# The triangular inverse carried through the lower rows on GpSimd or VectorE, with one joining product on TensorE, and decay products that run over two chunks

## The chip, the cores and the metric

The kernel runs on one core of one Trainium2 chip. The metric is the device time of one execution in microseconds (us). The kernel before took 593.81 us, the median of three runs (589.45 to 594.18).

## The reference

For 4 batches, 8 heads, 768 steps and head size 40, a state matrix is carried step by step; what comes out goes through a layer norm and a two-layer network of width 320 to 1280 to 320 with a residual.

```python
for t in range(S):
    y[:, :, t] = np.einsum('bhd,bhde->bhe', rt, state)
    Sa = np.einsum('bhde,bhe->bhd', state, at)
    state_decay = state * wt[:, :, None, :] - np.einsum('bhd,bhe->bhde', Sa, bt)
    state = state_decay + np.einsum('bhd,bhe->bhde', vt, kt)
...
ch = np.maximum(xn @ w_ch1, 0.0) @ w_ch2
return x + ch
```

The decays `w` lie between 0.85 and 0.95. All is float32.

## The kernel before

Time is cut into 24 chunks of C = 32 steps; B = 16 is half a chunk. The 32 pairs of batch and head lie in two halves of the partitions. Within a chunk the recurrence becomes matrix products and the inverse of a unit lower triangle of 32 x 32 for each pair.

For each chunk c there are these steps. `prep(c)` loads the decays `wa` and the rows `bk`, makes running products of the decays in the chunk (VectorE scan L338 from the front into `gE`, reciprocal L340, scan L342 from the back into `qE`), multiplies them into `x2s` (L350) and `bk` (L356), and forms the 32 x 32 interactions on TensorE (L366). Their signed copy goes by DMA to DRAM (`d_l`). Steps L350 and L356 are on VectorE for chunks 0 and 1, later on GpSimd (POOL in the profile).

`invert(s)` works on a slab: chunk 0 alone, chunk 1 alone, then two chunks at a time (11 slabs of two). The triangles come back from `d_l` into the tile `yv`, one pair of batch and head on each partition, and both 16 x 16 blocks on the diagonal are inverted at the same time in 14 steps of two instructions (L416 multiplies, L420 adds). Slabs 0 and 1 do this on VectorE, the others on POOL. ScalarE (ACT) copies a transposed block (L422), DMAs write `d_h`, and `merge(c)` reads it back into `hv`. There TensorE joins the two blocks: a first product (L441) makes a 16-column piece, ACT copies it into `qm` (L443), and a second product (L452) gives the whole inverse, which ACT copies to `tt`.

`chain(c)` is the recurrence from chunk to chunk: L498 from the state `x2`, a copy on ACT, L508 with the inverse `tt`, four copies on ACT (L512), L523, and then VectorE adds the old state (L532) and scales the sum by the decay product of the next chunk (L533), four times each. `post(c)` forms the output of the chunk (L551, L563, L578, L595). `norm` and `moe` are the layer norm and the network: L766 and L750 are its two products, done for two chunks at a time: ten groups of 8 matmuls (L766) and ten of 6 (L750).

The order of all instructions is set before the program is built. `Plan.order` is given each step with its engine, a cost in us, a key (the chunk, with an offset) and what it reads and writes; it lays the steps out as a list scheduler would and issues them in that order. At run time each engine takes its instructions strictly in that order, and an instruction that waits holds up all that stand behind it on its engine. A change of a cost therefore moves other steps too.

Of the kernel before, what the change touches and what calls it, by code (L numbers as in the profile page):

```python
# [11 lines left out]
F32 = mybir.dt.float32  # L12
# [4 lines left out]
ALU = mybir.AluOpType  # L17
# [4 lines left out]
C = 32  # L22
B = C // 2
D = 40
# [158 lines left out]
def body(ctx, tc, ea, eb, vr, rd, vt, w1, w1x_in, w2, gl, fe, fd, out):  # L183
# [27 lines left out]
    start0, = ring(1, "start0", 16, 33)  # L211
# [7 lines left out]

    yv, = ring(1, "yv", 2 * 33 * B)  # L220
    tmp, = ring(1, "ytmp", 2 * 56)

    hv = ring(2, "hv", 8, 5 * B)
    qm, = ring(1, "qm", 8, C)
# [23 lines left out]
    d_h = [dr.tile([32 * n, B, 3 * B], F32, name=f"d_h{s}") for s, (_, n) in enumerate(SLABS)]  # L248
# [15 lines left out]
    def consts():  # L264
# [16 lines left out]
        for i in range(2):  # L281

            op("DVE", 0.9, -99 + i, (), [("wa", i, 0)], lambda i=i: V.memset(wa[i][32:64], 1.0))
        for i in range(BK):
            op("POOL", 0.9, -99 + i, (), [("bk", i, 0)], lambda i=i: G.memset(bk[i][32:64], 1.0))
        op("POOL", 0.3, -84, (), ["qm"], lambda: G.memset(qm, 0.0))
# [5 lines left out]
        def f():  # L292
            V.memset(start0, 2.0 ** -33)
            V.memset(start0[:, :, 0:1], 1.0)
            V.memset(last, 0.0)
        op("DVE", 1.0, -95, (), ["start0", "last"], f)
        op("ACT", 0.3, -95, (), [("small", 0)], lambda: (A.memzero(small[0]["sd"]), A.sqrt(small[0]["sd"], small[0]["sd"])))
        for i in range(2):
# [3 lines left out]
            def f(i=i):  # L302
                for q, qs in enumerate(QUADS):
                    up, lo = (ident[qs, 32 * q + B * x:32 * q + B * x + B].unsqueeze(1).broadcast_to([32, 8, B])
                              for x in range(2))
                    A.copy(out=hv[i][qs, :, 0:B], in_=lo)
                    A.copy(out=hv[i][qs, :, 4 * B:5 * B], in_=up)
                    if i == 0:
                        A.copy(out=qm[qs, :, 0:B], in_=lo)
            op("ACT", 2.6 if i == 0 else 1.8, -50 + i, ["ident"], two("hv", i, 4) + (["qm"] if i == 0 else []), f)  # L310
# [13 lines left out]
    def prep(c):  # L324
# [9 lines left out]
        for hf in (1, 0):  # L334
# [3 lines left out]
        op("DVE", 1.35, kp, W + ["start0"], [("g", i)], lambda: nc.vector.tensor_tensor_scan(  # L338
            out=flat(g[R]), data0=t[R, 0:n], data1=flat(start0[R]), initial=0.0, op0=ALU.mult, op1=ALU.max), lock=True)
        op("DVE", 0.29, kp, [("g", i)], ["last"], lambda: nc.vector.reciprocal(  # L340
            out=last[R, :, C:33], in_=g[R, :, C:33]))
        op("DVE", 1.4, kp, W + ["last"], [("q", i)] + ([("go",)] if c == 0 else []), lambda: nc.vector.tensor_tensor_scan(  # L342
            out=flat(q[R])[:, ::-1], data0=t[R, n:0:-1], data1=flat(last[R])[:, ::-1], initial=0.0,
            op0=ALU.mult, op1=ALU.max), lock=True)
# [624 lines left out]
```

## Time and profile before

| | before |
|---|---|
| runs, median (range) | 593.81 us (589.45 to 594.18) |
| the profiled execution, its time | 596.33 us |
| its span, first to last instruction | 594.6 us |
| mean granted TensorE clock | 0.961 |
| TensorE (PE) busy | 517.6 us, 87% |
| VectorE (DVE) busy | 410.9 us, 69% |
| ScalarE (ACT) busy | 311.2 us, 52% |
| GpSimd (POOL) busy | 276.2 us, 46% |

In rows of groups stand the line, the engine, the operation, what is written and read, the shapes and the count; then the busy time in us, the mean ns of one, and the idle time before them with what ended it. One float32 matrix product of the program shows as two matmuls in the profile, so a block of 32 shows as 64. In rows of a timeline stand the start and the duration in us, and in square brackets the idle time of the engine before it. "issue" is a wait for which the profile shows no releaser. SPq is the queue of SyncE, which issues all DMAs of the kernel; its rows show the issue of a DMA, not its transfer.

### The profile page before, as it was taken

Reading aid. Unit: us, or ns where it says so; the run is one execution under the profiler, and the core shown is the slowest. Engines: PE = TensorE matmul, PEld = TensorE weight load, DVE = VectorE, ACT = ScalarE, POOL = GpSimd, SP = SyncE. Lnnn points to the kernel's source line nnn. Section 1 sums busy time; section 2 is a strip of 40 time slices with the busy share of each in tenths; the row PEclk is TensorE's granted clock in tenths of the full one; section 3 lists DMA queues with packets and bytes.
Section 4 is the critical chain, followed back from the end, with each engine's and each line's share of the span. In section 5 each row is a group of like instructions: output and inputs, shape, how many; then the busy total and the mean of one; then the engine's idle time right before and its main releaser. Section 6 shows DMA issues by size and latency. Waiting matters only on the chain.

```text
span 594.6 us, 33557 instructions
## 1 busy us (share of the span) xinstructions
PE 517.6 (87%) x14902; PEld 469.0 (79%) x14902; DVE 410.9 (69%) x907; ACT 311.2 (52%) x790; POOL 276.2 (46%) x510
## 2 busy tenths in 40 slices
PE   2527988799989899999899899899799899799996
PEld 2426766788879799888898798789799798688995
DVE  6699787787766667766676577686587667578622
ACT  8535768475465274373555365546456544555321
POOL 9425273374665572854824644674736706200000
PEclk9999779899989799998999899999999999899999
DMA  5465554425532435334243334434343344432000
GB/s 155 113 175 154 164 163 131 112 66 127 114 81 76 105 72 112 89 96 109 70 99 95 87 76 100 106 78 117 63 100 107 83 106 104 105 98 80 3 23 26
DMA packets 119670, 58.58 MB, mean 99 GB/s; under 512 B 100576, under 2 KB 106720, under 8 KB 119520
## 3 DMA queue, kind: packets, MB, share of 16 engines
q1 hardware_dynamic: 119520, 56.39, 38.6%
q8 instruction: 118, 1.93, 1.3%
q14 instruction: 32, 0.26, 0.1%
HBM read 44.56 MB, written 9.44 MB: 91 GB/s over the span
## 4 chain that ended last, share of the span: by engine, by line
PE 66%; POOL 8%; DVE 7%; issue 7%; ACT 5%; DMA 5%; SPq 1%; POOLq 0%; ACTq 0%; DVEq 0%
PE bank L750 17%; PE bank L766 16%; PE bank L366 4%; PE bank L578 4%; POOL ytmp L416 4%; POOL yv L420 4%; PE bank L595 2%; PE bank L498 2%; PE bank L508 2%; PE bank L441 2%; PE bank L452 2%; PE bank L563 2%; PE bank L473 2%; PE bank L523 2%; PE bank L551 2%
## 5 line engine op out<-in xcount | busy, mean ns | idle before, releaser
L750 PE MATMUL bank<-w,hh 128*128 128x320 f32 x480 | 119.9, 335 | 0.6 <-issue 0.6
L766 PE MATMUL bank<-xh,w 128*128 128x256 f32 x480 | 109.7, 290 | 4.4 <-issue 2.5
L769 ACT ACTIVATE hh<-bank 128x256 fp32r<-128x256 f32 x120 | 45.9, 384 | 116.4 <-PE bank L766 115.3
L771 DVE SCALAR_TENSOR_TENSOR hl<-bank,hh 128x256 fp32r<-128x256 f32 x120 | 49.9, 421 | 70.0 <-ACT hh L769 68.6
L766 PEld LDWEIGHTS bank<-xh,w 128*128 128x128 f32 x480 | 84.3, 193 | 4.4 <-issue 2.6
L750 PEld LDWEIGHTS bank<-w,hh 128*128 128x128 f32 x480 | 79.4, 195 | 7.6 <-issue 3.8
L356 POOL TENSOR_TENSOR bk<-bk,gE 104x1024 f32<-104x1024 f32 x22 | 48.9, 2222 | 65.7 <-issue 26.6
L750 PE MATMUL bank<-w,hl 128*128 128x320 f32 x240 | 76.2, 317 | 1.6 <-issue 1.6
L766 PE MATMUL bank<-xl,w 128*128 128x256 f32 x240 | 68.7, 286 | 0.2 <-issue 0.2
L350 POOL TENSOR_TENSOR x2s<-wa,qE 40x512 f32<-40x512 f32 x44 | 54.7, 1244 | 20.3 <-DVE qE L342 17.8
L420 POOL TENSOR_TENSOR yv<-yv,ytmp 64x28 f32<-64x28 f32 (+6 forms) x154 | 54.5, 354 | 12.1
L416 POOL TENSOR_TENSOR ytmp<-yv 64x28 f32<-64x28 f32 (+6 forms) x154 | 54.5, 354 | 11.4
L483 POOL MEMSET x5s<- 64x512 f32 x48 | 25.1, 522 | 71.6 <-PE bank L595 69.7
L532 DVE TENSOR_TENSOR bank<-bank,x 40x320 f32<-40x320 f32 x88 | 44.0, 500 | 11.2 <-PE bank L523 5.7
L478 ACT COPY xk<-bank 64x320 f32<-64x320 f32 x96 | 40.2, 419 | 21.7 <-PE bank L473 19.8
L584 DVE TENSOR_TENSOR x5s<-bank,mask 64x256 f32<-64x256 f32 x96 | 40.5, 422 | 15.4 <-PE bank L578 11.6
L766 PEld LDWEIGHTS bank<-xl,w 128*128 128x128 f32 x240 | 46.5, 194 | 3.1 <-issue 1.7
L750 PEld LDWEIGHTS bank<-w,hl 128*128 128x128 f32 x240 | 46.8, 195 | 1.4 <-issue 1.4
L512 ACT COPY x<-bank 32x320 f32<-32x320 f32 x96 | 40.1, 417 | 14.1 <-PE bank L508 12.8
L533 DVE TENSOR_TENSOR x<-bank,x2s 40x320 f32<-40x320 f32 x92 | 44.9, 489 | 3.1
L566 ACT COPY xk<-bank 40x320 f32<-40x320 f32 x96 | 40.2, 418 | 4.7 <-PE bank L563 3.0
L338 DVE TENSOR_TENSOR_SCAN gE<-wa,start 104x528 f32<-104x528 f32 x24 | 31.3, 1305 | 8.5 <-DMA wa<-in_ea_dram 4.8
(130 smaller groups left out, 1071.2 us busy)
## 6 DMA issues: line engine op xcount, KB each, us to landing
wa<-in_ea_dram SPq DMA_DIRECT2D x48, 162.7 KB
bk<-in_eb_dram SPq DMA_DIRECT2D x48, 160.0 KB
wa<-in_ea_dram SPq DMA_DIRECT2D x24, 165.0 KB
x<-in_vt_dram SPq DMA_DIRECT2D x48, 80.0 KB
x5s<-in_rd_dram SPq DMA_DIRECT2D x48, 80.0 KB
vu<-in_vr_dram SPq DMA_DIRECT2D x48, 80.0 KB
out_dram<-ot SPq DMA_DIRECT2D x24, 160.0 KB
r<-in_w_dram SPq DMA_DIRECT2D x10, 320.0 KB
```

Source lines behind the costliest of these rows:

```text
L350: op(eng, 0.75 * us, kp, W + [("q", i)], [("x2a", x, hf)], lambda hf=hf, rs=rs: e.tensor_tensor(out=x2s[x][rs, hf, 0:512].rearrange("p (h ...
L356: op(eng, 1.25 * us, kp, [("g", i)], K, lambda: e.tensor_tensor(out=kb, in0=kb, in1=g[R, :, 0:C].unsqueeze(2).broadcast_to([104, 16, 2, C] ...
L416: e.tensor_tensor(out=tv, in0=yb[:, :, j + 1:, j:j + 1].broadcast_to(S), in1=yb[:, :, j:j + 1, 0:j].broadcast_to(S), op=ALU.mult)
L420: e.tensor_tensor(out=v, in0=v, in1=tv, op=ALU.add)
L478: op("ACT", 0.45, c - 1.2 + 0.1 * bb, [bs[hf]], [X[hf]], lambda b=bs[hf], zs=zs, hf=hf, bb=bb: nc.scalar.copy(out=xk[i][zs, hf, 8 * bb:8 * ...
L532: nc.vector.tensor_tensor(out=p, in0=p, in1=x2[i][rs, hf, ps], op=ALU.add)
L533: nc.vector.tensor_tensor(out=x2[o][rs, hf, ps], in0=p, in1=x2s[xo][rs, hf, 512 + 8 * bb:520 + 8 * bb].unsqueeze(2).broadcast_to([D, 8, D] ...
L584: op("DVE", 0.46, k + 0.5, [b, "mask"], [("z", i)], lambda b=b, zs=zs, ps=ps, hf=hf, bb=bb: nc.vector.tensor_tensor(out=x5s[i][zs, hf, 8 * ...
L750: mm(bank_of(po[u])[:, 0:CH], lhsT=l[:, us], rhs=ws[f"w2_{f // 2}"][:, f % 2, x], start=f == 0 and n == 0, stop=f == 9 and n == 2)
L766: mm(ph, lhsT=l, rhs=r, start=n == 0, stop=n == 7)
L769: yield "ACT", 0.39, [phs[f]], [("hh", f % 2)], lambda f=f: nc.scalar.activation(out=hht[f % 2], in_=bank_of(phs[f])[:, 0:256], func=AF.Re ...
L771: yield "DVE", 0.46, [phs[f], ("hh", f % 2)], [("hl", f % 2)], lambda f=f: nc.vector.scalar_tensor_tensor(out=hlt[f % 2], in0=bank_of(phs[ ...
```

## The change

Three things change.

1. The inverse. `yv` now holds each triangle twice, on twice as many partitions: a left copy with all 32 rows, and a right copy that starts at row 16, column 16 (a second, shorter DMA). 15 steps instead of 14 run over the first 16 columns, and each goes down through all rows below, so that the left copy ends with the upper inverse and, below it, the lower left block already multiplied by it. One step works on (31 - j) x j elements on each partition (30 to 240) instead of 2 x (15 - j) x j (28 to 112). The two halves are written to `d_h` by two DMAs, in pieces of 16 numbers (before: one DMA with pieces of 32 numbers at this place, and one from `d_l` that was issued earlier). `merge` reads 32 partitions of 8 x 32 numbers instead of 16 of 8 x 48, and has one product (L453) and no copy to `qm`.
2. The decays. The scan from the back comes first. For an odd chunk it starts from the product of the whole even chunk before it (a small VectorE copy, L341), so the products run over two chunks. The scan from the front starts from its reciprocal.
3. The state. An even chunk only adds (L539), an odd one adds and scales (L540). Chunk 0 copies on ACT (L534). The 16-column copies of the decay product to `x2s` (L359) are made for odd chunks only.

The core of the diff:

```diff
-        op("DVE", 1.35, kp, W + ["start0"], [("g", i)], lambda: nc.vector.tensor_tensor_scan(
-            out=flat(g[R]), data0=t[R, 0:n], data1=flat(start0[R]), initial=0.0, op0=ALU.mult, op1=ALU.max), lock=True)
...
+        if h:
+            op("DVE", 0.15, kp, [("q", 0)], [("start", 1)], lambda: nc.vector.tensor_copy(
+                out=start[1][R, :, C:33], in_=qE[0][R, :, 0:1]))
...
+        op("DVE", 1.35, kp, W + ["last"], [("g", i)], lambda: nc.vector.tensor_tensor_scan(
+            out=flat(g[R]), data0=t[R, 0:n], data1=flat(last[R]), initial=0.0, op0=ALU.mult, op1=ALU.max), lock=True)
...
-        dma(k0, 262, L, Y, y[:, 0:1024], d_l[s].rearrange("m a t -> m (a t)"))
-        op(eng, 0.15, k0, (), Y, lambda: e.memset(y[:, 0:1024:33], 1.0))
...
-        for j in range(1, B - 1):
-            m = B - 1 - j
-            S = [n, 2, m, j]
...
+        dma(k0, 131 * n // 32, L, [(*q, 0) for q in Y], yl[:, 0:1024], tri)
+        dma(k0, 64 * n // 32, L, [(*q, 1) for q in Y], yr[:, 0:1024 - 33 * B], tri[:, 33 * B:1024])
...
+        for j in range(1, B):
+            m = C - 1 - j
+            S = [2 * n, m, j]
...
-            op(eng, us, k0 + 0.02 * j, (), Y, f, lock=True)
...
+            op(eng, 0.23 + 0.0021 * m * j if dve else 0.4 + 0.0036 * m * j, k0 + 0.02 * j, (), Y, f, lock=True)
...
+        dma(k0 + 0.4, 100 * n // 32, Y, [("d_h", s, 1)], d_h[s][:, :, B:C], rows(yl)[:, :, 0:B], 1024)
+        dma(k0 + 0.4, 100 * n // 32, Y, [("d_h", s, 0)], d_h[s][:, :, 0:B], rows(yr)[:, :, B:C], 1024)
...
-                    mm(po[qs, h], lhsT=hv[i][qs, h, 0:2 * B], rhs=hv[i][qs, h, 3 * B:4 * B], start=True, stop=True)
-        op("PE", 0.66, km, two("hv", i, 4), [b], f, opens=[b], room=["qm"], recs=64.5)
-        op("ACT", 0.29, km, [b], ["qm"], lambda b=b: nc.scalar.copy(
...
-                    mm(po[qs, h], lhsT=qm[qs, h], rhs=right[qs, h], start=True, stop=True)
+                    mm(po[qs, h], lhsT=hv[i][qs, h, 0:C], rhs=hv[i][qs, h, C:2 * C], start=True, stop=True)
...
+                        elif c % 2 == 0:
+                            nc.vector.tensor_tensor(out=to, in0=p, in1=old, op=ALU.add)
```

The old cost of a step of the inverse was 0.54 us on VectorE and 0.9 us on POOL. In the order three places matter.

TensorE before, around the joining of chunk 17 (L441 and L452; `hv_91` holds its blocks, L578 belongs to chunk 16, L498 opens the recurrence of chunk 17):

```order
3188 L441 MATMUL bank_147<-hv_91 32x16 x32
3189 L578 MATMUL bank_146<-x5s_101,vu_105 64x2x32 x16
3190 L452 MATMUL bank_145<-hv_91,qm_92 32x32 x32
3191 L498 MATMUL bank_148<-x_1_96,x2s_98 32x40 x32
3192 L750 MATMUL bank_151<-w_0_1131,hh_138 128x320 x2
```

TensorE now, at the same chunk (L453 is the one product, L584 is the former L578, L499 the former L498, L601 the former L595, L772 and L756 the former L766 and L750):

```order
3170 L772 MATMUL bank_149<-xl_137,w1x 128x256
3171 L453 MATMUL bank_147<-hv_92 32x32 x32
3172 L584 MATMUL bank_146<-x5s_101,vu_105 64x2x32 x16
3173 L499 MATMUL bank_145<-x_1_96,x2s_98 32x40 x32
3174 L601 MATMUL bank_148<-xk_103,x5s_101 32x40 x32
```

The block L441 is gone here and at the other 23 chunks. Between the end of L366 of a slab's second chunk and the first joining product of that slab there stood, on the mean of the 11 slabs of two chunks, 7.7 groups of L766 and 7.6 of L750; now there are 9.1 and 8.9.

ScalarE before, around the copy that ends the inverse of chunks 16 and 17 (L422); behind it stand copies for the network and the output (L737, L554, L769):

```order
485 L769 ACTIVATE hh_139<-bank_149 128x256
486 L422 COPY yv_88<-yv_88 64x16x16
487 L737 CAST xh_135<-bank_150 128x3x128
488 L554 COPY vu_106<-bank_148 40x16x32
489 L554 COPY vu_106<-bank_146 40x16x32
490 L769 ACTIVATE hh_138<-bank_149 128x256
```

ScalarE now, at the same slab (L434 is the former L422, L513 the former L512, L775 the former L769):

```order
452 L734 COPY xn_118<-xn_118 128x64
453 L513 COPY x_1_96<-bank_148 32x320
454 L434 COPY yv_89<-yv_89 64x16x16
455 L513 COPY x_1_96<-bank_148 32x320 x2
456 L775 ACTIVATE hh_138<-bank_150 128x256
457 L743 CAST xh_135<-bank_149 128x3x128
458 L513 COPY x_1_96<-bank_148 32x320
```

The copy that waits for POOL now stands among the four copies that the recurrence needs.

VectorE now, at the start of the program (L343 and L348 are the scans, L375 the former L369; L649, L650 and L652 convert the network's weights and before stood behind both inverses; L419 opens the inverse of slab 0):

```order
18 L355 TENSOR_TENSOR x2s_98<-wa_78,qE_85 40x512 x2
19 L362 TENSOR_TENSOR bk_80<-bk_80,gE_83 104x1024
20 L649 TENSOR_SCALAR bank_149<-bank_149 128x320
21 L650 SCALAR_TENSOR_TENSOR bank_149<-rx,bank_149 128x320
22 L652 SCALAR_TENSOR_TENSOR ot_142<-rx,bank_149 128x320
23 L375 TENSOR_TENSOR gk_87<-bank_147,sign_73 128x512
24 L649 TENSOR_SCALAR bank_150<-bank_150 128x320
25 L650 SCALAR_TENSOR_TENSOR bank_150<-rx,bank_150 128x320
26 L652 SCALAR_TENSOR_TENSOR ot_142<-rx,bank_150 128x320
27 L419 MEMSET yv_89 64x16
```

VectorE before, at the same place:

```order
16 L350 TENSOR_TENSOR x2s_98<-wa_77,qE_84 40x512 x2
17 L356 TENSOR_TENSOR bk_79<-bk_79,gE_82 104x1024
18 L369 TENSOR_TENSOR gk_86<-bank_147,sign_73 128x512
19 L408 MEMSET yv_88 32x32
20 L416 TENSOR_TENSOR ytmp_89<-yv_88 32x28
```

Six conversions have moved ahead of the two inverses on VectorE.

113 lines of the change are left out of this document (56 added, 57 removed).

## The prediction

> **What bounds the kernel now.** I read the page first, then the busy time by stage.
>
> ```profile
> span 594.6 us, 33557 instructions
> PE 517.6 (87%) x14902; PEld 469.0 (79%) x14902; DVE 410.9 (69%) x907; ACT 311.2 (52%) x790; POOL 276.2 (46%) x510
> q1 hardware_dynamic: 119520, 56.39, 38.6%
> PE 66%; POOL 8%; DVE 7%; issue 7%; ACT 5%; DMA 5%; SPq 1%; POOLq 0%; ACTq 0%; DVEq 0%
> ```
>
> ```profile
> 0.00:60.00 60.00, 26.98 (x928) 23.62 (x930) 47.88 (x116) 33.37 (x83) 32.40 (x53) 1.00 0.57 149
> 60.00:130.00 70.00, 60.66 (x1422) 49.97 (x1419) 54.77 (x109) 47.28 (x113) 35.17 (x74) 0.85 0.49 130
> 130.00:540.00 410.00, 382.29 (x11863) 349.68 (x11860) 282.88 (x621) 215.25 (x555) 208.62 (x384) 0.97 0.40 94
> 540.00:594.00 54.00, 47.71 (x704) 45.76 (x702) 25.42 (x64) 15.32 (x41) 0.00 (x0) 0.99 0.11 33
> ```
>
> The columns after a stretch's length are the busy us of PE, PEld, DVE, ACT and POOL, then the clock and the DMA share. From 130 to 540 us PE is busy 382.29 of 410: TensorE sets the pace, and work taken from it is time, provided that nothing makes it wait longer. In the first 60 us it is busy 26.98; there VectorE has 47.88. The second question is thus what PE waits for in the long stage.
>
> ```profile
> PE bank L441 <- issue: 3.5, 2, 2.7
> PE bank L766 <- issue: 2.7, 5, 1.1
> PE bank L452 <- issue: 2.1, 2, 1.9
> PE bank L498 <- DVE x L533: 0.7, 1, 0.7
> ```
>
> These (130 to 540 us) are three of the longest, and the only one for VectorE's scaling. No joining product waits for its data here, so today the inverses come in time. But POOL is 8% of the chain that ended last, and the waits of the whole run say how it gets there:
>
> ```profile
> ACT yv L422 <- POOL yv L420: 11.4, 4, 4.9
> ```
>
> In four slabs ScalarE stood at the inverse's closing copy until POOL was done, and all that PE needs from ScalarE stood behind it.
>
> **The change part by part.** The sum is made against the profiled execution, 596.33 us (span 594.6), 2.5 above the runs' median of 593.81.
>
> ```profile
> L452 PE MATMUL bank<-hv,qm 32*32 32x32 f32 x1536 | 19.5, 199 | 3.5 <-issue 2.1 <-ACT vu L554 0.9 <-ACT qm L443 0.5
> L441 PE MATMUL bank<-hv 32*32 32x16 f32 x1536 | 19.3, 183 | 16.6 <-DMA hv<-d_h 12.2 <-issue 3.5 <-ACT vu L554 0.7
> L533 DVE TENSOR_TENSOR x<-bank,x2s 40x320 f32<-40x320 f32 x92 | 44.9, 489 | 3.1
> L443 ACT COPY qm<-bank 128x128 f32<-128x128 f32 x24 | 6.4, 265 | 7.9 <-PE bank L441 7.7
> L420 POOL TENSOR_TENSOR yv<-yv,ytmp 64x112 f32<-64x112 f32 x22 | 9.4, 428 | 1.7
> L416 POOL TENSOR_TENSOR ytmp<-yv 64x28 f32<-64x28 f32 x22 | 6.0, 274 | 1.1
> L420 DVE TENSOR_TENSOR yv<-yv,ytmp 32x112 f32<-32x112 f32 x4 | 1.1, 263 | 0.1
> L416 DVE TENSOR_TENSOR ytmp<-yv 32x28 f32<-32x28 f32 x4 | 0.7, 174 | 1.5 <-issue 1.4
> ```
>
> ```profile
> 414.97 0.72 PE L441 MATMUL bank<-hv 32*32 32x16 f32 x64
> 415.63 1.15 PE L578 MATMUL bank<-x5s,vu 104*64 104x64 f32 x32
> 416.71 0.75 PE L452 MATMUL bank<-hv,qm 32*32 32x32 f32 x64
> 417.39 0.73 PE L498 MATMUL bank<-x,x2s 96*32 96x40 f32 x57
> ```
>
> (1) *One product less.* The next block starts 0.66 us after L441 (414.97 to 415.63). 24 x 0.66 = 15.8 us off PE. By busy time it is 19.3, since the early blocks are longer; I take **-15.8**. The product that stays has the form of L452 and costs what L452 costs.
>
> (2) *Waits marked "issue".* Those before L441 and L452 sum to 5.6 us. They sit at blocks of many small matmuls, and 24 of these go. Ends 0 and -5.6; **-2**.
>
> (3) *ScalarE and VectorE.* L443 goes (6.4 us), the scaling falls from 92 to 44 instructions (48 x 0.489 = 23.5 us of VectorE), and four adds move to ScalarE in chunk 0. In the long stage VectorE is busy 282.88 of 410, and PE waited for L533 once, 0.7 us: hidden under PE, **0** (to -1). The scans change places and one small copy is added for an odd chunk; the decay work of a chunk stays one scan, a reciprocal, a scan.
>
> (4) *The start.* Slabs 0 and 1 are inverted on VectorE.
>
> ```profile
> 38.49 1.46 PE L441 MATMUL bank<-hv 32*32 32x16 f32 x64 [12.23 <-DMA hv<-d_h]
> 40.47 1.08 PE L452 MATMUL bank<-hv,qm 32*32 32x32 f32 x64 [0.53 <-ACT qm L443]
> 48.16 1.05 PE L441 MATMUL bank<-hv 32*32 32x16 f32 x64 [0.72 <-ACT vu L554]
> 58.75 0.63 PE L508 MATMUL bank<-hn,tt 32*32 32x40 f32 x47 [3.41 <-issue]
> ```
>
> ```profile
> L643 DVE TENSOR_SCALAR bank<-bank 128x320 uint32<-128x320 uint32 x12 | 5.9, 490 | 0.3 <-ACT bank L638 0.2
> ```
>
> A step's instruction there takes 0.174 us at 28 elements and 0.263 at 112, so 0.144 + 0.00106 per element, and 28 of them with 2240 elements take 6.4 us. The new 30 have 2 x 2480 = 4960 elements: 4.3 + 5.3 = 9.6 us, +3.2 a slab, 6.4 for both. Against that, chunk 0 no longer needs the first product and its copy (38.49 to 40.47, 2.0 us), and chunk 1 likewise 1.0 or more. Six conversions of 0.49 us (L643 and its two kin) now stand ahead of the inverses, and leave the place behind them. PE is idle half of this stage, and 3.41 us of it fall before chunk 1's L508 anyway. Ends -1 and +6.4; **+2**.
>
> (5) *The inverse on POOL, 11 slabs.*
>
> ```profile
> 374.10 0.16 POOL L408 MEMSET yv<- 64x32 f32 x1 [4.75 <-ACT xk L566]
> 386.31 0.23 POOL L420 TENSOR_TENSOR yv<-yv,ytmp 64x28 f32<-64x28 f32 x1
> 89.56 1.76 SPq L260 DMA_DIRECT2D hv<-d_h  x4
> 95.73 0.73 PE L441 MATMUL bank<-hv 32*32 32x16 f32 x64
> 511.45 2.75 SPq L260 DMA_DIRECT2D hv<-d_h  x4
> 520.69 0.73 PE L441 MATMUL bank<-hv 32*32 32x16 f32 x64
> ```
>
> From 374.10 to 386.54 one takes 12.4 us. By the two POOL rows an instruction costs 0.22 + 0.00183 per element (428 at 112, 274 at 28), and the gaps add some 0.07: 30 x 0.29 + 4960 x 0.00183 = 8.7 + 9.1 = 17.8 us, against 28 x 0.29 + 2240 x 0.00183 = 12.2 by the same rule: **+5.6 us of delay**. That the new ones run on 128 partitions and not 64 is free if POOL goes by elements on a partition, as in L356 (104 x 1024 in 2.22 us):
>
> ```profile
> L356 POOL TENSOR_TENSOR bk<-bk,gE 104x1024 f32<-104x1024 f32 x22 | 48.9, 2222 | 65.7 <-issue 26.6
> ```
>
> The write to `d_h` goes from 1024 pieces to 4096 a slab. Its least cost is the second issue, 0.6 us. Its most is 3072 more pieces at the mean of all packets (38.6% x 16 x 594.6 us / 119520 = 31 ns), over 16 engines: 5.9 us. Small pieces are below that mean, so I take +2.5. The second load of `yv` and the wider load of `hv` go beside the first. Together 8.1 us more from `d_l` to `merge`.
>
> The order gives some of it back. With 1.4 more groups of L766 and 1.3 of L750 ahead of the first joining product, at 0.95 and 1.08 us,
>
> ```profile
> 395.13 1.08 PE bank L750 x6
> 396.20 0.95 PE bank L766 x8
> ```
>
> that is 2.7 us, with other blocks some 4. Slack is there too: from the end of a chunk's four `hv` issues to L441 there were 4.4 us in the first of the 11 slabs (91.32 to 95.73) and 6.5 in the last (514.20 to 520.69). I set 2 aside for the landing of the last one; at least 2.5 are free. 8.1 - 4 - 2.5 leaves 1.6 us a slab, 18 in all. Part of it only replaces waits that PE has in these 410 us anyway (27.7 idle): I take half, **+9**; ends 0 and +25. The way it is paid is named above: ScalarE stands at the closing copy, now L434, and behind it stand L513, which the recurrence needs, and the network's L775.
>
> POOL rises by 11 x 5.6 = 62 us to 338 and does not become a bound by its sum. SyncE issues one DMA more a slab.
>
> Sum: -15.8 - 2 + 0 + 2 + 9 = -6.8. 596.3 - 6.8 = 589.5 in the profiled execution, **587** by the runs' median.
>
> A rule speaks against part (5). The Trainium skill, GPSIMD Engine Reference, section 3.1, puts a two-input operation at about 2.6 cycles of 1.2 GHz for each element; as an estimate that is 2.2 ns, where the rows here give 1.83. By it the inverse would take 8.7 + 10.8 = 19.5 us and the sum, halved as above, would be +2. The trace holds no step of over 112 elements, so it is kept as a rival below.
>
> **The rivals.**
>
> *The longer inverse is hidden.* All of (5) fits into slack. For it: no joining product waited for data in the long stage. Against: the four waits at L422. -15.8 - 2 + 2 = -15.8, in runs **578**.
>
> *Late inverses hold ScalarE and PE.* Place: L434 in ScalarE's order and L453 in PE's. If the write of `d_h` costs 5.5 and not 2.5, 4.6 us a slab are left, half of them 2.3: 25 us. -15.8 - 2 + 2 + 25 = +9.2, in runs **603**. It decides from about 2 us lost a slab ((15.8 + 6) / 11). For it: the share of POOL in the chain, and L422's longest wait of 4.9 us. Against: PE has two output tiles of network work between the recurrence's blocks.
> The Trainium skill bears on its condition: DMA: Bandwidth & Descriptors, Specifications, says that transfers under 512 B are read, changed and written back. No row here shows a 64 B write from SBUF.
>
> *Gain and loss cancel.* POOL's larger steps go at L356's gross rate (2222 / 1024 = 2.17 ns): 8.7 + 10.8 = 19.5 us, 1.7 more a slab than taken, half of it 9 in all. -6.8 + 9 = +2, in runs **596** with the rest as forecast. The page named under (5) would have it so.
>
> That the change does not do what it says is out: the 24 blocks are gone from PE's order.
>
> **How the numbers follow.** Forecast 0.42 (its own range 580 to 594), hidden 0.25, held 0.20, cancelled 0.13. A measurement here can tell about 1%, 6 us: faster is below 588, slower above 600. Of the forecast somewhat over half lies below 588: faster 0.25 + 0.25 = 0.50. Same: 0.17 + 0.13 = 0.30. Slower: 0.20. The range reaches from the best ends (-15.8 - 5.6 - 1 + 2 = -20.4, in runs 573) to the middle of the held case: 573 to 604.
>
> **What would show it.** Right: 24 blocks on the one joining line, PE's busy time near 500 us, POOL's near 338; steps of 240 elements near 0.66 us; L434 waiting for POOL in more than four slabs, for more than 11.4 us in all; PE's idle time between 130 us and the last chunk some 8 us above 27.7. The hidden case shows no such waits, the held case PE idle before L453 or behind L434 by over 2 us a slab. Wrong altogether: PE's blocks longer by a lower clock (0.961 now), or a first network group far later than in the profile before.

## The result, and the profile after

| | before | after |
|---|---|---|
| runs on one chip, median (range) | 591.63 us (588.64 to 594.18) | 622.12 us (620.67 to 623.01) |
| ratio to before, 95% interval | | 1.0515 (1.0449 to 1.0581) |
| span of the profiled execution | 594.6 us | 618.7 us |
| mean granted TensorE clock | 0.961 | 0.900 |

The change makes the kernel 5% slower. 622 us lies above the predicted range of 573 to 604. The two profiled executions are 24 us apart (596.33 and 620.67 us) and not 30, since the one of before was longer than the median of its runs. The page of the changed kernel, its first line on the engines, the DMA queue and the chain that ended last:

```profile
PE 510.7 (83%) x13366; PEld 462.3 (75%) x13366; DVE 406.8 (66%) x878; ACT 303.6 (49%) x742; POOL 346.1 (56%) x543
q1 hardware_dynamic: 157360, 59.48, 40.3%
PE 43%; POOL 26%; issue 8%; DMA 7%; DVE 7%; ACT 5%; SPq 4%; POOLq 0%; DVEq 0%; ACTq 0%
```

TensorE has 1536 matmuls fewer, but is busy only 6.9 us less (517.6 to 510.7), and its part of the chain falls from 66% to 43%. What took its place is GpSimd: 26%, from 8%. By stages (length, then busy us of PE, PEld, DVE, ACT and POOL, then clock and DMA share):

```profile
0.00:60.00 60.00, 21.21 (x545) 17.71 (x547) 49.61 (x104) 31.93 (x74) 29.41 (x50) 0.73 0.56 144
60.00:130.00 70.00, 58.08 (x1287) 48.20 (x1283) 55.51 (x106) 41.91 (x96) 45.71 (x70) 0.79 0.54 135
130.00:540.00 410.00, 360.50 (x10231) 328.90 (x10227) 261.10 (x570) 202.93 (x505) 269.93 (x423) 0.93 0.42 96
```

In the long stage PE now stands idle 49.5 of 410 us, where it was 27.7, and its clock is 0.93 where it was 0.97. The waits of ScalarE, TensorE and VectorE over the whole run:

```profile
ACT yv L434 <- POOL yv L432: 35.5, 11, 6.3
ACT yv L434 <- DVE yv L432: 13.0, 2, 8.5
PE bank L453 <- DMA hv<-d_h: 16.4, 1, 16.4
PE bank L372 <- POOL bk L362: 11.2, 5, 6.6
PE bank L524 <- ACT x L513: 6.2, 3, 5.4
DVE hl L777 <- ACT hh L775: 105.1, 70, 6.1
```

ScalarE now stands at the closing copy in all eleven slabs of GpSimd, 35.5 us (11.4 in four before). The joining product L453 itself waits for its data only once, in the start. What stands is what lies behind ScalarE (L524, for example), and, a second way, the interactions L372, which wait for the keys' product L362 on GpSimd. One slab shows the first way. The timeline, GpSimd's last steps, then ScalarE, TensorE and the queue of SyncE:

```profile
401.81 0.65 POOL L432 TENSOR_TENSOR yv<-yv,ytmp 128x238 f32<-128x238 f32 x1
402.49 0.62 ACT L434 COPY yv<-yv 64x256 f32<-64x256 f32 x1 [5.68 <-POOL yv L432]
403.14 0.84 ACT L513 COPY x<-bank 32x320 f32<-32x320 f32 x2
403.23 0.65 POOL L432 TENSOR_TENSOR yv<-yv,ytmp 128x240 f32<-128x240 f32 x1
403.90 1.64 SPq L261 DMA_DIRECT2D d_h<-yv  x2
405.26 1.74 PE L524 MATMUL bank<-x,xk 64*40 64x40 f32 x64 [5.36 <-ACT x L513]
408.98 4.66 SPq L261 DMA_DIRECT2D hv<-d_h  x8
```

ScalarE waits 5.68 us for the last step that the copy needs. Only then come three of the four copies L513, and L524, which reads them, finds PE idle for 5.36 us. The stall costs more than its own length, since PE comes back slow:

```profile
397.58 0.28 PE L772 MATMUL bank<-xh,w 128*128 128x256 f32 x1
397.70 0.28 PE L772 MATMUL bank<-xh,w1x 128*128 128x256 f32 x1
...
408.16 0.41 PE L772 MATMUL bank<-xh,w 128*128 128x256 f32 x1
408.38 0.41 PE L772 MATMUL bank<-xh,w1x 128*128 128x256 f32 x1
...
411.48 0.28 PE L772 MATMUL bank<-xh,w 128*128 128x256 f32 x1
411.60 0.28 PE L772 MATMUL bank<-xh,w1x 128*128 128x256 f32 x1
```

The same product starts every 0.12 us before the stall, every 0.22 us after it, and every 0.12 us again from 411.00 us on, 5.7 us after PE took up work. The Trainium skill, TensorE: Matmul & The Clock Gate, section "What's actually happening", has a gate that halves the clock after an idle window of about 3.4 us and opens after as long a busy one; the trace agrees with the slowing (0.22 against 0.12 us, after 5.36 us idle) and, more loosely, with the return (after 5.7 us).

### The profile page after: what moved, and what is told of

It is laid out like the page before. It is cut to its first block, busy times and chain, and to the rows that moved or that the text cites. A ratio compares the mean times of both kernels' runs of the same rounds, so it can differ in the third digit from the quotient of the medians.

```text
span 618.7 us, 30498 instructions
## 1 busy us (share of the span) xinstructions
PE 510.7 (83%) x13366; PEld 462.3 (75%) x13366; DVE 406.8 (66%) x878; ACT 303.6 (49%) x742; POOL 346.1 (56%) x543
## 4 chain that ended last, share of the span: by engine, by line
PE 43%; POOL 26%; issue 8%; DMA 7%; DVE 7%; ACT 5%; SPq 4%; POOLq 0%; DVEq 0%; ACTq 0%
POOL yv L432 11%; POOL ytmp L429 11%; PE bank L756 11%; PE bank L772 11%; DMA yv<-d_l 4%; SPq L261 4%; PE bank L372 3%; PE bank L584 3%; PE bank L499 2%; PE bank L569 2%; PE bank L695 2%; PE bank L453 2%; PE bank L601 1%; PE bank L474 1%; PE bank L524 1%
## 5 line engine op out<-in xcount | busy, mean ns | idle before, releaser
L756 PE MATMUL bank<-w,hh 128*128 128x320 f32 x480 | 120.5, 337 | 2.9 <-issue 2.9
L772 PE MATMUL bank<-xh,w 128*128 128x256 f32 x480 | 111.4, 294 | 3.0 <-DVE xl L744 3.0
L775 ACT ACTIVATE hh<-bank 128x256 fp32r<-128x256 f32 x120 | 46.1, 384 | 117.1 <-PE bank L772 116.2
L432 POOL TENSOR_TENSOR yv<-yv,ytmp 128x30 f32<-128x30 f32 (+4 forms) x165 | 90.1, 546 | 12.9
L429 POOL TENSOR_TENSOR ytmp<-yv 128x30 f32<-128x30 f32 (+4 forms) x165 | 85.5, 518 | 13.0
L772 PEld LDWEIGHTS bank<-xh,w 128*128 128x128 f32 x480 | 85.8, 197 | 4.5 <-DVE xl L744 3.3
L756 PEld LDWEIGHTS bank<-w,hh 128*128 128x128 f32 x480 | 80.6, 198 | 5.7 <-issue 1.9
L756 PE MATMUL bank<-w,hl 128*128 128x320 f32 x240 | 76.5, 319 | 0.8 <-DVE gk L375 0.8
L355 POOL TENSOR_TENSOR x2s<-wa,qE 40x512 f32<-40x512 f32 x44 | 53.1, 1207 | 32.0 <-DVE qE L343 29.5
L772 PE MATMUL bank<-xl,w 128*128 128x256 f32 x240 | 69.3, 289 | 0.0
L362 POOL TENSOR_TENSOR bk<-bk,gE 104x1024 f32<-104x1024 f32 x22 | 49.8, 2263 | 33.1 <-DMA bk<-in_eb_dram 18.7
L590 DVE TENSOR_TENSOR x5s<-bank,mask 64x256 f32<-64x256 f32 x96 | 40.5, 422 | 13.8 <-PE bank L584 11.4
L756 PEld LDWEIGHTS bank<-w,hl 128*128 128x128 f32 x240 | 47.2, 197 | 2.8 <-issue 1.2
L772 PEld LDWEIGHTS bank<-xl,w 128*128 128x128 f32 x240 | 47.3, 197 | 0.0
L372 PE MATMUL bank<-x2s,bk 104*64 104x64 f32 x768 | 32.6, 249 | 17.7 <-POOL bk L362 11.2
L513 ACT COPY x<-bank 32x320 f32<-32x320 f32 x96 | 40.1, 417 | 9.5 <-PE bank L509 8.0
L372 PEld LDWEIGHTS bank<-x2s,bk 104*64 104x64 f32 x768 | 29.4, 161 | 20.4 <-POOL bk L362 12.4
L343 DVE TENSOR_TENSOR_SCAN qE<-wa,start 104x528 f32<-104x528 f32 x24 | 32.1, 1336 | 7.7 <-DMA wa<-in_ea_dram 3.8
```

What stands on the lines that cost most here:

```text
L355: op(eng, 0.75 * us, kp, W + [("q", i)], [("x2a", x, hf)], lambda hf=hf, rs=rs: e.tensor_tensor(out=x2s[x][rs, hf, 0:512].rearrange("p (h ...
L362: op(eng, 1.25 * us, kp, [("g", i)], K, lambda: e.tensor_tensor(out=kb, in0=kb, in1=g[R, :, 0:C].unsqueeze(2).broadcast_to([104, 16, 2, C] ...
L372: mm(pg[64 * bb:64 * bb + 64, :, h], lhsT=tb[R, 64 * p:64 * p + 64], rhs=x2s[x][R, :, 32 * p:32 * p + 32], start=True, stop=True)
L429: e.tensor_tensor(out=tv, in0=yb[:, j + 1:, j:j + 1].broadcast_to(S), in1=yb[:, j:j + 1, 0:j].broadcast_to(S), op=ALU.mult)
L432: e.tensor_tensor(out=v, in0=v, in1=tv, op=ALU.add)
L590: op("DVE", 0.46, k + 0.5, [b, "mask"], [("z", i)], lambda b=b, zs=zs, ps=ps, hf=hf, bb=bb: nc.vector.tensor_tensor(out=x5s[i][zs, hf, 8 * ...
```

## The experiments

Each run was compared with the kernel before on the same chip. The kernel before had medians of 591 to 599 us from chip to chip, so effects below are differences of ratios times 592 us; by the intervals, such a difference is uncertain by 5 to 7 us.

### Which part of the change

The changed kernel with only the inversion put back (functions `invert` and `merge` of before, and their tiles), and the kernel before with only the inversion changed:

```diff
 only_decay:   after  - invert, merge of after   + invert, merge of before
 only_inverse: before - invert, merge of before  + invert, merge of after
```

> Only the decays over two chunks and the state scaled once a pair; inverse and joining as before. Theory A (the longer way from the interactions to the joining product, by the inverse on POOL and the write of d_h, makes PE wait): 588 to 594 us, like before. Rival B (the new decay scheme is what costs, by its copies on VectorE and the later product of bk): 605 us or more. Rival C (the start on VectorE): like A.

> Only the inverse through the lower rows with one joining product; decays and state as before. A: 615 to 625 us, the whole loss. B: 600 us or less.

only_decay: 590.17 us, ratio 1.0001 (0.9956 to 1.0046). only_inverse: 620.68 us, 1.0512 (1.0399 to 1.0625). The whole loss is the inversion's. The scheme of the decays costs and gains nothing that these runs can tell.

### The length of the inverse

Steps 8 to 15, 12 to 15, or 14 and 15 left out on GpSimd's slabs, so that the inverse stays unfinished there; the other instructions keep their order.

```diff
             def f(j=j, m=m, S=S):
+                if not dve and j > 7:      # pool_half; pool_cut4: 11, pool_cut2: 13
+                    return
                 tv = tmp[p0:p0 + 2 * n, 0:m * j].rearrange("p (a t) -> p a t", t=j)
```

> The changed kernel in its own order, but steps 8 to 15 of the inverse are left out on POOL (11 slabs), so the inverse is not finished there. They take 8 x 0.55 + 1752 x 0.0038 = 11 us a slab in the trace of the changed kernel. A: PE's waits after 130 us fall from 49 us to 25 or less and the time to 590 to 600 us. B or C: 612 us or more, since neither is touched.

> The changed kernel with steps 12 to 15 of the inversion left out on GpSimd's slabs (the output is then not the reference's; the order of all other work is kept). By the trace of the changed kernel these four steps take 5.8 of a slab's 18 us, so that the inverse is about as long as the one of the kernel before. Two forms of the theory that the long way from interactions to joining product makes TensorE wait: (a) each microsecond of the way costs alike, as leaving out about 10.7 us a slab gave 44.9: 622 - 44.9 x 5.8/10.7 = 598, 592 to 604; (b) the way costs only past a point, and at 12 us of inverse all of it is hidden: 576 to 583. A time above 612 would say that the last steps are not what counts, and that the saving of the half inversion came from something else, as GpSimd being free for its other work early in a chunk.

> The changed kernel with only steps 14 and 15 left out on GpSimd's slabs, 2.9 us of a slab's inverse by the trace (the inversion is left unfinished). With four steps out (5.8 us) the time was 579, with eight out 577, so the cost bends somewhere. If it rises evenly from the 579 kernel to the changed one: 600, 595 to 606. If there is a point past which everything tips over, it is either still 578 to 588 or already 614 to 622.

| kernel | POOL busy | median | ratio (95% interval) |
|---|---|---|---|
| pool_half | 232.9 us | 577.26 us | 0.9765 (0.9683 to 0.9848) |
| pool_cut4 | 285.8 us | 579.37 us | 0.9753 (0.9672 to 0.9835) |
| pool_cut2 | 315.2 us | 601.07 us | 1.0161 (1.0035 to 1.0286) |
| after | 346.1 us | 622.12 us | 1.0515 (1.0449 to 1.0581) |

pool_half came out faster than the 590 to 600 us expected, and the other two runs show why: there is a bend. Up to an inverse as long as the one before the change (pool_cut4: 60.3 us of GpSimd less, 5.5 a slab), length is free: the last 53 us that pool_half takes away bring nothing. From there on each slab's 5.5 us cost 0.0762 x 592 = 45.1 us in all, 4.1 a slab, and pool_cut2 lies about halfway. The profile of pool_cut4, busy time of the long stage and the chain:

```profile
130.00:540.00 410.00, 384.03 (x11224) 350.02 (x11222) 289.13 (x631) 222.64 (x553) 220.12 (x347) 0.98 0.45 104
PE 62%; DVE 11%; DMA 9%; issue 6%; ACT 5%; POOL 3%; SPq 3%; DVEq 0%; POOLq 0%; ACTq 0%
ACT yv L436 <- POOL yv L434: 2.5, 3, 1.4
```

GpSimd leaves the chain (3%), ScalarE hardly waits for it (L436 is the closing copy there), PE's clock is back at 0.98 and its idle time at 26.0 us.

### Length of the way, or load of GpSimd

Leaving steps out does two things: the inverse is ready sooner, and GpSimd has less to do. Here the steps 12 to 15 stay, but on scratch:

```diff
+                if not dve and j > 11:
+                    tv = tmp[p0:p0 + 2 * n, 0:m * j]
+                    e.tensor_tensor(out=tv, in0=tv, in1=tv, op=ALU.mult)
+                    e.tensor_tensor(out=tv, in0=tv, in1=tv, op=ALU.add)
+                    return
```

> The changed kernel in its own order, with steps 12 to 15 of GpSimd's slabs still executed with the same sizes, but on a scratch tile that nobody reads, so that the inverse of a slab ends after step 11 while GpSimd stays as busy as in the changed kernel (the inversion is left unfinished). It parts two things that leaving the steps out changed together. If the length of the way from the interactions to the joining product costs: near the 579 of that run, 577 to 588. If it is GpSimd's load, which makes the other work on GpSimd late (L362 for the interactions, L355, the memsets): 608 to 624. In between, both carry a part in proportion.

601.09 us, ratio 1.0153 (1.0061 to 1.0245): neither theory alone. GpSimd is busy 341.7 us, nearly as in the changed kernel. Of the 45 us, 0.0362 x 592 = 21 are the longer way and 0.0400 x 592 = 24 the load, each uncertain by about 7 us and taken in this order (first the way shortened, then the load). TensorE's and ScalarE's waits for GpSimd in this run:

```profile
PE bank L372 <- POOL bk L362: 20.9, 7, 4.5
ACT yv L439 <- POOL yv L437: 1.9, 2, 1.4
```

ScalarE is free again (L439 is the copy), but the interactions wait 20.9 us for the keys' product, which stands behind the inverse's steps in GpSimd's order; 1.3 us with the steps left out. The next run takes that product away from GpSimd, in the run with scratch steps (load_keys) and in the changed kernel itself (keys_dve):

```diff
-        op(eng, 1.25 * us, kp, [("g", i)], K, lambda: e.tensor_tensor(
+        op("DVE", 1.25, kp, [("g", i)], K, lambda: nc.vector.tensor_tensor(
```

> The run with steps 12 to 15 of GpSimd's slabs on scratch (inverse ready after step 11, GpSimd as busy as in the changed kernel; the inversion is left unfinished), and the keys' product (L362) on VectorE besides. With the short way but GpSimd as busy, TensorE waited 20.9 us for that product, 7 times, and the time was 601 against 579 with the steps left out. If the load half works through this wait: 578 to 590. If the wait only moves to GpSimd's other product (L355) or VectorE's 1.3 us a chunk takes its place: 597 to 610.

> The changed kernel with the product of the keys with the decays (L362) on VectorE in place of GpSimd for all chunks; what is computed is the same. It takes about 2.4 us a chunk from GpSimd's queue, where it stands behind a whole inverse and ahead of the interactions (L372, which waited 20.9 us for it in the run with scratch steps), and gives VectorE 1.3 us a chunk. If GpSimd's load works through this wait: 600 to 610. If the load works elsewhere, or VectorE's new work costs as much: 616 to 630.

load_keys: 592.59 us, 0.9999 (0.9947 to 1.0052). keys_dve: 613.18 us, 1.0300 (1.0223 to 1.0376). The waits of load_keys (L458 is the joining product):

```profile
PE bank L372 <- POOL x2s L355: 6.6, 3, 4.0
PE bank L372 <- POOL ytmp L434: 2.6, 1, 2.6
PE bank L458 <- DMA hv<-d_h: 22.1, 6, 16.1
SPq L261 <- POOL x2s L355: 22.5, 6, 6.0
```

The wait shrinks and moves: to GpSimd's next product, L355, and to the joining product (16.1 us of its 22.1 are the wait in the start). 9 of the 24 us of the load go (0.0154 x 592), with 1.3 us a chunk more on VectorE; in the changed kernel 13 of 30 (0.0215 x 592). The rest of the load half is not one wait of PE. The last row shows a way that it can take: SyncE stands at a load of decays until L355 on GpSimd has read the old ones, and each of these six times the reads of `hv` stand a few places behind that load in SyncE's order. In pool_load, with the same wait (20.0 us in six), 9.0 us pass from the first issue of the write of `d_h` to the first issue of its read, in pool_cut4 7.0 (mean of nine slabs). So what is called load here is in part a longer way again; how large that part is stays open.

### Where ScalarE stands

The closing copy on the engine that inverts, for all slabs (copy_self), or for GpSimd's slabs alone (copy_pool):

```diff
-        op("ACT", 0.5, k0 + 0.4, (), Y, lambda: nc.scalar.copy(
+        op(eng, 0.4 if dve else 0.7, k0 + 0.4, (), Y, lambda: e.tensor_copy(
             out=rows(yr)[:, B:C, B:C], in_=rows(yr)[:, 0:B, 0:B].rearrange("p a k -> p k a")))
```

> The changed kernel, with the closing copy of the inverse on the engine that inverts instead of on ScalarE. If it is ScalarE standing at that copy (35.5 us in 11 waits) that PE pays for: 600 to 612 us. If PE waits because the data come late at the joining product: 616 us or more, since the way gets no shorter.

> The changed kernel with the closing copy of the inverse (L434) on GpSimd for GpSimd's slabs, and on ScalarE as it is for the two of VectorE; what is computed is the same. In the run with the copy on the inverting engine for all slabs the inverse was applied every 41.8 us a pair of chunks after the start, against 44.6 in the changed kernel, but the start was 15 us later. If the shorter period belongs to the copy, and the late start to the two copies on VectorE: about ten pairs by 2.9 us less, 622 - 29 = 593, 588 to 601, level with the kernel before. If the period came with the late start (work put off from the start fills the gaps later): 610 to 620.

copy_self: 616.69 us, 1.0414 (1.0326 to 1.0502). copy_pool: 617.7 us, 1.0308 (1.0228 to 1.0388). TensorE's longest waits of copy_pool (L454 is the joining product):

```profile
PE bank L372 <- POOL bk L362: 32.8, 9, 6.2
PE bank L454 <- DMA hv<-d_h: 20.9, 7, 15.8
```

ScalarE is no longer held by GpSimd, and by the ratios 6 us (not told apart from none) and 12 us come back. The rest did not go; it changed its place. Now PE itself waits, at the interactions (32.8 us against 11.2) and at the joining product (seven times, not once). ScalarE's wait shows where the loss appears, but most of the loss stays without it. The expected 593 us did not come: copy_pool starts its chunk 4 as early as the changed kernel (154.1 and 154.0 us), and its pair of chunks takes 45.2 us, not 41.8. That copy_self's shorter pair came with its late start fits this, but no run tests it.

One place none of these runs takes away: SyncE, which issues all DMAs in order, stands at the write of `d_h` until GpSimd is done, and loads of later chunks stand behind it. The waits of its queue for GpSimd's last steps in pool_cut4, in the changed kernel and in copy_pool:

```profile
SPq L261 <- POOL yv L434: 0.7, 3, 0.4
SPq L261 <- POOL yv L432: 39.8, 7, 9.6
SPq L261 <- POOL yv L432: 60.3, 12, 9.4
```

With the copy gone from ScalarE, SyncE waits 20 us more. No run gives the writes a queue of their own, so what this wait costs stays open.

### The write of the inverse, the start, the planner's costs

```diff
 dh_whole
-        dma(k0 + 0.4, 100 * n // 32, Y, [("d_h", s, 1)], d_h[s][:, :, B:C], rows(yl)[:, :, 0:B], 1024)
-        dma(k0 + 0.4, 100 * n // 32, Y, [("d_h", s, 0)], d_h[s][:, :, 0:B], rows(yr)[:, :, B:C], 1024)
+        dma(k0 + 0.4, 100 * n // 32, Y, [("d_h", s, 1)], d_h[s].rearrange("m a t -> m (a t)"), yl[:, 0:1024], 1024)
+        P.add("SP", 0.35 + 1024 * 0.0006, lambda: None, k0 + 0.4, Y, [("d_h", s, 0)], kb=100 * n // 32)
 dve_half
+                if dve and j > 7:
+                    return
 true_cost
-            op(eng, 0.23 + 0.0021 * m * j if dve else 0.4 + 0.0036 * m * j, k0 + 0.02 * j, (), Y, f, lock=True)
+            op(eng, 0.39 + 0.0020 * m * j if dve else 0.55 + 0.0039 * m * j, k0 + 0.02 * j, (), Y, f, lock=True)
-        100 * n // 32 in both writes of d_h
+        400 * n // 32
```

> The changed kernel with the inverse written to DRAM by one DMA of whole 4 KB rows in place of two DMAs of 64-byte pieces (what lies in the right half of the columns is then not the reference's). By the traces the small pieces make the way from issue of the write to the first read of it 5.2 to 7.2 us, against 2.7 to 4.4 before the change, so some 3 us a slab go. If the length of the way is what costs: 622 - 44.9 x 3/10.7 = 609, 603 to 614. If the transfers hide beside the inverse of the next slab: 619 to 624.

> The changed kernel with steps 8 to 15 of the inversion left out on the two first slabs alone, those on VectorE (output not the reference's; order of the other work kept). Those steps are about 6 of the 10.8 us that each of the two inverses takes. If the start carries its own share of the loss (the first inverse is applied 8.7 us later than before the change): 622 less 6 to 12 gives 610 to 616. If the start is made up for later, since the chain of waits is set by GpSimd's slabs: 619 to 623.

> The changed kernel with the planner's costs of the inversion's steps raised to what the trace shows (0.39 + 0.0020 us an element on VectorE, 0.55 + 0.0039 on GpSimd) and of the write of the inverse raised fourfold; only the order of the instructions differs. If the loss comes from an order made with costs that are too small: 600 to 612. If it comes from the length of the way itself, which no order shortens: 617 to 626.

| kernel | median | ratio (95% interval) | against after |
|---|---|---|---|
| dh_whole | 617.15 us | 1.0410 (1.0322 to 1.0497) | -6 us |
| dve_half | 619.42 us | 1.0446 (1.0358 to 1.0534) | -4 us |
| true_cost | 623.10 us | 1.0485 (1.0367 to 1.0602) | -2 us |

All three intervals overlap that of the changed kernel, so none is told apart from it; if dh_whole and dve_half give something back, it is a small share. dh_whole also shortened less than was meant: from the issue of the write to the first read 5.2 us pass (mean of nine slabs), 6.1 in the changed kernel and 3.4 before. With true costs the long stage got better (PE busy 370.65 against 360.50 of 410 us), but the first stretch worse; PE waits 22.6 us at L394 there, once:

```profile
PE bank L394 <- ACT qc L395: 31.1, 2, 22.6
```

### Other work on VectorE, more buffers, an earlier start

These compute all that the changed kernel computes, and were meant to buy the loss back: every second two-chunk slab inverted on VectorE (alt); one buffer more in the rings of `bk` and `x2s` (buf); the same with preparation and inversion due half a chunk earlier (lead_buf), with the keys' product on VectorE besides (keys_lead), and buf with the closing copy on GpSimd (copy_pool_buf).

```diff
 alt        -        dve = c0 < 2            +        dve = c0 < 2 or c0 % 4 == 0
 buf        -BK = 3                          +BK = 4
            -XS = 4                          +XS = 5
 lead_buf   -        kp = c - 3.4 - soon(c)  +        kp = c - (3.9 if c > 3 else 3.4) - soon(c)
            -        k0 = c0 - 2.0 - 2 * soon(c0)
            +        k0 = c0 - (2.5 if c0 > 3 else 2.0) - 2 * soon(c0)
```

> The changed kernel with the inversion of every second two-chunk slab (the five that begin at chunks 4, 8, 12, 16, 20) on VectorE in place of GpSimd; what is computed is the same. An inverse on VectorE took 10.7 us against 18, so five of eleven slabs get a way shorter by 7 us, and VectorE gets 54 us more work. If the way costs slab by slab: 622 - 43 x 5/11 = 602, 595 to 608. If one long way in four chunks is enough to hold the whole line up, or VectorE's new work stands before the subtractions that the networks wait for: 610 to 630.

> The changed kernel with one buffer more in two rings, four for the keys that the preparation of a chunk writes and five for its left factors; what is computed is the same. If those rings tie the preparation of a later chunk to the end of an earlier one, and the longer way has used up what they allowed: 585 to 608. If the order written by the planner, not the buffers, decides when the preparation comes: 615 to 626.

> The changed kernel with the preparation of a chunk and the inversion of a slab due half a chunk earlier from chunk 4 on, and one buffer more in the two rings that this needs; what is computed is the same. If the length of the way counts for half of the loss, and can be bought back by an earlier start: 22 us less or more, 595 to 603; below 590 if GpSimd's own lateness is cured by it too. If the earlier start only shifts GpSimd's load and its queue stays as full: 612 to 622.

> Both edits of the two runs beside it at once: the preparation and the inversion half a chunk earlier with one buffer more, and the keys' product on VectorE. What is computed is the same. If way and load each carry half of the loss and the edits answer one each: 578 to 592, at or below the kernel before. If only one of them does: within 4 us of the better of the two runs.

> The same, with one buffer more in the two rings besides; what is computed is the same. The one buffer alone brought the period from 44.6 to 41.7 us and the fourth chunk's application 6 us later. If the two shorten the same stretch, a floor is TensorE's own 40.6 us a pair as in the runs with the steps left out: 588 to 600. If neither holds without its late start: 608 to 620.

| kernel | median | ratio (95% interval) |
|---|---|---|
| alt | 643.12 us | 1.0812 (1.0691 to 1.0933) |
| buf | 617.91 us | 1.0439 (1.0341 to 1.0536) |
| lead_buf | 610.57 us | 1.0261 (1.0196 to 1.0325) |
| keys_lead | 616.62 us | 1.0311 (1.0225 to 1.0398) |
| copy_pool_buf | 615.57 us | 1.0298 (1.0230 to 1.0365) |

lead_buf gives back 15 us, half of the 30 lost against before, and so the buffers and due times do bind a part of it. The remedies do not add up: keys_lead is no better than keys_dve alone (neither expected case covers its time), and copy_pool_buf is no better than copy_pool. alt is worst, above every range expected for it, though GpSimd falls to 267.0 us busy:

```profile
PE 519.6 (81%) x13366; PEld 468.1 (73%) x13366; DVE 465.4 (73%) x1038; ACT 302.1 (47%) x742; POOL 267.0 (42%) x383
ACT yv L434 <- DVE yv L432: 26.3, 5, 9.0
ACT yv L434 <- POOL yv L432: 22.2, 6, 6.3
```

ScalarE stands for VectorE's slabs as it does for GpSimd's, 48.5 us in all. That VectorE's other work, late behind the inverses, adds to it is likely but not shown. No version that keeps the new inversion whole beat the kernel before; how far an order made anew could go was not settled.

### One measure for these runs

From the traces: the way from the end of the later chunk's interactions (L372, before L366) to the use of the inverse in the slab's first chunk (L509, before L508), mean of the nine slabs from chunk 4 to 20, and the time from pair to pair of chunks, from L509 of chunk 4 to that of chunk 20 over eight.

| kernel | way | a pair of chunks | L509 of chunk 4 starts |
|---|---|---|---|
| before | 48.6 us | 43.1 us | 144.5 us |
| after | 49.7 us | 44.6 us | 154.0 us |
| pool_cut2 | 47.7 us | 42.4 us | 154.9 us |
| pool_load | 48.5 us | 42.9 us | 152.7 us |
| load_keys | 47.1 us | 42.8 us | 150.0 us |
| pool_cut4 | 46.2 us | 40.6 us | 155.8 us |
| pool_half | 46.0 us | 40.6 us | 150.0 us |
| buf | 49.5 us | 41.7 us | 159.8 us |
| lead_buf | 53.1 us | 43.1 us | 166.9 us |

In the first seven rows a longer way goes with a longer pair: from pool_cut4 to after 3.5 us of way and 4.1 of pair. The spans of these two are 38.2 us apart; 32.5 of them lie in the eight pairs, 7.5 behind L509 of chunk 20, and -1.8 ahead of chunk 4. That the way sets the pair is argued from this, not shown, and the last two rows go against it: buf keeps the way of after with a pair 2.9 us shorter, lead_buf has the longest way and a pair of 43.1. Both start late, and their times follow the pair only in part.

## Why the prediction was wrong, step by step

**(1) One product less, -15.8, and (2) the issue waits, -2: the gain came, in a size that agrees partly by luck.** pool_cut4 has the changed kernel's work but for an inverse no longer than before, and it runs at 0.9753: 14.6 us less, where (1), (2) and the start's +2 make 15.8. That is the time of the rival "hidden" (578). The gain is there; it shows only where the inverse is in time. By the traces of before and pool_cut4 two errors cancel in it: PE's busy time fell by 19.0 us and its waits marked "issue" in the long stage from 16.4 to 10.3, together more than the 17.8 of the sum, while L509 of chunk 4 came 11.3 us late. In the changed kernel PE was busy 6.9 us less, not the 18 that the sign "PE's busy time near 500" asked for, since what remained ran at a lower clock; with the steps left out it is 498.6.

**(3) ScalarE and VectorE, 0: right.** only_decay is at 1.0001. PE waited for L533 in the long stage of before twice and not once (0.5 us more, at L563), which changes nothing.

**(4) The start, +2: open, and perhaps too small.** Chunk 4's L509 came 9.5 us later than before. How much of that is lost at the end is not settled. In dve_half this L509 comes 5.5 us earlier than in the changed kernel (148.5 us) and the profiled span is 5.6 us shorter, as if it were lost in full; its runs put the gain at 4 us, which is not told apart from 0. On the other side only_decay starts 4.7 us later than before and is not slower.

**(5) The inverse on GpSimd, +9 (ends 0 and +25): this step failed.** Its first half held. An inverse took 17.5 to 20.4 us (17.8 predicted), against 11.5 to 13.2. From the end of the interactions to the joining product the way grew from 36.5 to 43.6 us on average. These 7.1 are near the 8.1 of the sum, but not the same measure: the 8.1 are counted from `d_l`, and the 7.1 hold the work that moved ahead of the product. But the added length cost 45 us, 4.1 a slab, where the sum had 0.8 a slab. Two steps had it wrong.

The first is GpSimd's load, put at nothing: the prediction said that POOL "does not become a bound by its sum". That is true of the sum (346.1 of 618.7 us; 338 predicted), but in GpSimd's order an inverse is one piece of 18 us, and the products behind it (L355, L362) come late for the interactions of later chunks. With the way short and only the load kept, that is 24 us.

The second is the half taken off for waits that PE has anyway. The way alone is 21 us, 1.9 a slab, near the 1.6 that stood there before the halving. PE's idle time in the long stage rose by 21.8 us, and a stall is followed by a slow clock (the stage's 0.97 became 0.93), for which the sum had no term. That 1.6 came near is luck in part. "The order gives 4" was too small: from the joining product to L509 there are 6.1 us now and 12.1 before, so more work moved ahead. "At least 2.5 are free" was too large: it was read off the first and the last slab (4.4 and 6.5 us), and at the eleven slabs the same stretch runs from 1.7 to 8.0 us. At chunk 4 it is 134.58 to 136.40, less than the 2 us set aside for the landing:

```profile
132.53 2.05 SPq L260 DMA_DIRECT2D hv<-d_h  x4
136.40 0.73 PE L441 MATMUL bank<-hv 32*32 32x16 f32 x64
```

**The rival "late inverses hold ScalarE and PE"** (603, 0.20) named the place and the sign, L434 with eleven waits of 35.5 us, and the point from which it decides. It priced a slab at 2.3 us, half of 4.6; 4.1 was measured. It expected the size to hang on the write of `d_h`; dh_whole gives back 6 us, not told apart from none. And its mechanism is only part of it: with ScalarE freed 6 to 12 us came back, and SyncE, which waits for GpSimd too, it did not name.

**"Gain and loss cancel"** priced GpSimd at 2.17 ns an element. The rows of a small and a large step give less:

```profile
L429 POOL TENSOR_TENSOR ytmp<-yv 128x30 f32<-128x30 f32 x11 | 3.2, 294 | 0.9
L429 POOL TENSOR_TENSOR ytmp<-yv 128x238 f32<-128x238 f32 x11 | 6.8, 618 | 0.9
```

(618 - 294) / 208 = 1.56 ns. The rule of the Trainium skill, GPSIMD Engine Reference, section 3.1, weighed there as 2.2 ns, does not hold for these sizes.

**The signs.** 24 blocks on the joining line, POOL near 338 (346.1), L434 waiting in more than four slabs for more than 11.4 us: seen. A largest step near 0.66 us: 0.617 (L429) and 0.725 (L432). PE's idle time 8 us above 27.7: it was 21.8 above, 2.0 a slab, where the held case began. The lower clock that was set down as "wrong altogether" came, and the first network group began at 94.6 us, 86.9 before.

## What to carry to other kernels

Work taken from the bounding engine and laid on another one's longest dependent piece is priced by that piece's way to its consumer and by all that is queued behind it, on its engine and on the queues that wait for it, not by that engine's busy share. When the trace already shows another engine standing for that piece, take most of each added microsecond as lost (here 4.1 of 5.5), and add the slow clock after a stall. Read the slack at every slab, not at two. To measure such a price, leave out the added steps, and then run them on scratch: the first shows way and load together, the second parts them, as far as the load does not lengthen the way again.

## What the runs showed of the hardware

GpSimd and VectorE delay each other. Two GpSimd steps under a VectorE scan took more than twice as long (the timeline of the slab above):

```profile
395.11 0.59 POOL L429 TENSOR_TENSOR ytmp<-yv 128x220 f32<-128x220 f32 x1
395.47 1.34 DVE L343 TENSOR_TENSOR_SCAN qE<-wa,start 104x528 f32<-104x528 f32 x1
395.78 1.45 POOL L432 TENSOR_TENSOR yv<-yv,ytmp 128x220 f32<-128x220 f32 x1
397.21 1.26 DVE L348 TENSOR_TENSOR_SCAN gE<-wa,last 104x528 f32<-104x528 f32 x1
397.31 1.56 POOL L429 TENSOR_TENSOR ytmp<-yv 128x228 f32<-128x228 f32 x1
398.95 0.68 POOL L432 TENSOR_TENSOR yv<-yv,ytmp 128x228 f32<-128x228 f32 x1
```

1.45 and 1.56 us, against 0.59 and 0.68 beside them. Of the 330 steps of the run 11 overlapped a scan: five took 1.45 to 1.56 us, the other six at most 0.11 us more than is usual at their size, so that not every overlap costs. The other way round, the new 16-element copy on VectorE stands until GpSimd's running instruction has ended. The rows of such a copy, first with GpSimd at work, then without:

```profile
234.31 1.18 POOL L355 TENSOR_TENSOR x2s<-wa,qE 40x512 f32<-40x512 f32 x1
234.42 1.12 DVE L341 COPY start<-qE 104x16 f32<-104x16 f32 x1
370.64 0.17 DVE L341 COPY start<-qE 104x16 f32<-104x16 f32 x1
```

The twelve copies took 0.12 to 2.83 us; the nine that met a GpSimd instruction ended 0.04 or 0.05 us after one had ended. The Trainium skill, GPSIMD Engine Reference, section 8 (Key points), has GpSimd share its SBUF interfaces with VectorE, with contention for instructions of two SBUF inputs or in a two-port mode; the scans, with two inputs, agree with it. The copy has one input; whether it runs in such a mode no run here shows.
